# Block-masked attention with a mixture of experts behind it: earlier choice of the experts, one weight buffer split per pair

## The chip, the core and the metric

The kernel runs on one core of one Trainium2 chip. The metric is device time in microseconds (us); the median of three runs before the change is 755.88 us (754.58 to 757.23). Engines are named as in the profile: PE is TensorE, DVE is VectorE, ACT is ScalarE, POOL is GpSimd, SP is the engine whose queue issues most DMAs. L207 means line 207 of the kernel.

## The reference, cut to what matters

```python
# q, k, v: (8 batches, 8 heads, 576, 64)
scores = (1 / 8) * q @ k.T                  # per batch and head
scores = where(block_i >= block_j, scores, -1e9)        # blocks of 64, causal
attn = exp(scores - max); attn = attn / (attn.sum() + 1e-9)
x = (attn @ v)                              # as (4608, 512): a row per batch and position
logits = x @ w_gate + modality_bias[modality_id]        # 8 experts
e_idx = argmax(logits); gate_w = softmax(logits)[e_idx]
for e in range(8):                          # w1: 512 x 1024, w2: 1024 x 512 per expert
    rows = (e_idx == e)
    out[rows] = gate_w[rows] * (relu(x[rows] @ w1[e]) @ w2[e])
```

With the inputs of this problem nearly all rows go to two of the eight experts.

## The kernel before, in words

**Attention.** Two heads of a batch make a pair; there are 32 pairs, four to a batch. `run_slot` writes the order of one slot by hand, following the tuple ORDER, and every engine executes its instructions in the order in which they are written. In slot p the kernel makes for pair p the scores (S, L207, PE), the row maxima (M, L214, DVE), the exponentials (E, L227, ACT), the transposes (T, L234, PE, in six groups) and the copies of the transposes out of PSUM (C, L239; the tuple ON_DVE says which groups DVE copies, ACT copies the others). Beside this it finishes pair p-1: products with v (V, L253, PE), a copy of them (O, L261 and L262, ACT), the reciprocal of the row sums (D: `den`, L279, and L280, DVE), a turn back together with the product with w_gate (B, L273, PE), and the scaled rows (Z0 and Z1, L292 and L293, DVE). After Z1 of a batch's last pair SP stores that batch's rows (L299, eight DMAs).

**Scaling q.** q of pair p+1 is multiplied by 1/8 at "Q" of slot p: by DVE for pair 0, by ACT in one instruction for pairs from LATE = 25 on (L186), by POOL in four instructions of 144 columns for the others (L189). S of pair p+1 needs all of it. q and k of pair p+2 come with one DMA on SP's queue at "L" of slot p (L176), v of the next pair at the start of a slot (L179).

**Routing.** Z1 of a batch's last pair first empties the list `steps` of what is left in it and then fills it with the 18 steps of `routing`, small DVE instructions for the most part, with two products on PE (`total` and `counts`, only at "qp"), `biased` and `running` (only at "qv") and one exponential on ACT (`expo`). At q1 to q6 of a slot one step is executed, two in the slots 20 to 23 (slot // 4 == EARLY), and three while the next step is one of `choose`. `weight_out` turns the five sums of a partition into 80 weights (L377), which `stores` sends to `xrows` on SP. At the end five scatters per batch (L399, an indirect DMA that POOL issues) write the row numbers into `idlist`; they are made one by one at S0 and T0 of the following slots.

**Choosing two experts.** After the routing of batch EARLY - 1 = 4, 22 more DVE steps (`choose`) pick the two experts with the most rows so far, `a` and `b`, and compute where their lists begin. Of expert `a` the first 768 rows (NLEAD = 3 segments of 256) are fetched from the batches counted so far.

**Weights.** EARLY_STEPS says what is done for expert `a` before attention ends: "stage" loads a quarter of w1 or w2 (512 KB) into one of two staging buffers by SP's queue, and "prep" splits a buffer on POOL into a rounded part and a remainder, in four times a cast (L588) and a subtraction (L589) of 256 columns. "ids" and "fetch" load the list and gather the first rows. Eight buffers are split and ten staged in the slots 25 to 30.

**Experts.** The tuple LAST mixes the end of attention with the first segment's products; `run_all` then computes 18 segments, each with three fp32r products per matrix (L710 up, L756 down), ReLU and split on ACT and DVE (L716, L717), and an indirect DMA of the result (L759, POOL). `rest` would loop over what the covered segments leave.

Of the kernel before, what the change touches and what calls it, by code (L numbers as in the profile page):

```python
# [22 lines left out]
B, H, S, D = 8, 8, 576, 64  # L23
N, DM, NE, DF = 4608, 512, 8, 1024
NPAIR = B * H // 2
PPB = H // 2
NSUB = S // D
XW = 528
IW = 16
# [4 lines left out]
NROW = NE * REGION  # L34
COVER = SLOT * NSLOT
COVER_B = COVER - FEW
EARLY, NLEAD = 5, 3
LEAD = SLOT * NLEAD
BIG = float(1 << 20)
NWARM = 12  # L40
LATE = 25
SCALE = 0.125
GUARD = 1e-9
VW = D + NE
# [13 lines left out]
)  # L58
BLOCK = (12, 0, 8, 4, 16, 20)
POS = {x: BLOCK[g] + i for g, group in enumerate(GROUPS) for i, x in enumerate(group)}  # L60
ON_DVE = (0, 1, 3, 5)
SUMS = ((2, 4, 6, 5), (1, 3, 7, 8, 0))
TAILS = ((6, 3, 20, 0), (0, 5, 20, 1), (4, 2, 21, 0), (8, 4, 21, 1), (2, 1, 22, 0))
PRODUCTS = ((0, (5,)), (0, (1, 3, 7)), (0, (2, 4, 6)), (0, (8,)), (1, (4, 6, 5)), (1, (3, 7, 8)), (2, (6, 5)), (2, (7, 8)), (3, (7, 8)))
# [9 lines left out]
)  # L74

EARLY_STEPS = {
    (25, "S0"): ("stage", "stage"),
    (26, "S0"): ("prep",), (26, "T0"): ("stage", "prep"),
    (27, "S0"): ("stage", "prep"), (27, "T0"): ("stage", "prep"),
    (28, "S0"): ("ids", "stage", "prep"), (28, "T0"): ("stage", "prep"),  # L80
    (29, "S0"): ("stage", "prep"), (29, "T0"): ("stage", "prep"),
    (30, "S0"): ("fetch", "stage"), (30, "T0"): ("fetch",),
    (31, "S0"): ("fetch",), (31, "T0"): ("fetch",),
}
LAST = (
# [25 lines left out]
def attention_moe(ctx, tc, qk, vr, bkw, mid, mb, w1, w2, cf, ci, ld, out):  # L111
    nc = tc.nc
    pe, act, dve, pool = nc.tensor, nc.scalar, nc.vector, nc.gpsimd
# [64 lines left out]
    def load_v(p):  # L178
        nc.sync.dma_start(pairs[p].v.rearrange("p h a f -> p (h a f)"), vr[p])  # L179

    def scale(p):
        d = pairs[p]
        if p == 0:
            dve.tensor_scalar(d.q, d.raw[:, 0:S], SCALE, None, ALU.mult)
        elif p >= LATE:
            act.mul(d.q, d.raw[:, 0:S], SCALE)  # L186
        else:
            for i in range(0, S, 144):
                pool.tensor_scalar(d.q[:, i : i + 144], d.raw[:, i : i + 144], SCALE, None, ALU.mult)  # L189
# [46 lines left out]
    def copies(p, g):  # L236
        n = len(GROUPS[g])
        dst, src = pairs[p].pt[:, BLOCK[g] : BLOCK[g] + n].rearrange("p b c -> p (b c)"), banks[g][:, 0 : 128 * n]
        dve.tensor_copy(dst, src) if g in ON_DVE else act.copy(dst, src)  # L239

# [63 lines left out]
    def routing(b):  # L304
        xr, gl = xrs[b]
        g = Pair()
# [3 lines left out]
        def t(shape, dt=F32, **k):  # L310
            return sml.tile(shape, dt, bufs=2, **k)
# [3 lines left out]
        ix, pp, sm = (t([128, 5], name=n) for n in ("ix", "pp", "sm"))  # L315
# [58 lines left out]

        def weight_out():
            g.wt = t([128, 5, IW], name="wt")
            dve.reciprocal(g.wt, sm.unsqueeze(2).to_broadcast([128, 5, IW]))  # L377

        def stores():
            queue = nc.sync  # L380
# [12 lines left out]
        def place_sum():  # L393
# [10 lines left out]
            placing.extend((scatter, c) for c in range(5))  # L404

        return [logits, total, biased, top, shifted, hits, expo, hit_index, first, onehot, weight, weight_guard, weight_out, stores, counts, running, place_run, place_pick, place_sum]

    sel = {}
# [25 lines left out]
    def choose(eng):  # L434
        lead, start = (cst.tile([128, NE], F32, name=n) for n in ("taken", "start"))
        eng.tensor_tensor(cnt, run, bases, ALU.subtract)
        sel["oha"], sel["ea"] = pick(eng, cnt, "a", kx, ranks)
        oha = sel["oha"]
        eng.scalar_tensor_tensor(cnb, oha, -BIG, cnt, ALU.mult, ALU.add)
        eng.scalar_tensor_tensor(lead, cnt, float(LEAD), oha, ALU.min, ALU.mult)  # L440
        sel["ohb"], sel["eb"] = pick(eng, cnb, "b", kx, ranks)
        eng.tensor_tensor(rest, lead, bases, ALU.add)
        sel["ra"] = dot(eng, oha, bases, "a")
        sel["rr"] = dot(eng, oha, rest, "r")
        sel["rb"] = dot(eng, sel["ohb"], bases, "b")
        eng.scalar_tensor_tensor(begin, oha, float(COVER - LEAD), rest, ALU.mult, ALU.add)
        eng.scalar_tensor_tensor(start, sel["ohb"], float(COVER_B), begin, ALU.mult, ALU.add)
        sel["start"] = start

    def emit(name, p):  # L450
        one = {
            "L": lambda: load(p), "Q": lambda: scale(p), "V": lambda: values(p), "O": lambda: turn_out(p), "D": lambda: inverse(p), "B": lambda: back(p),
            "Z0": lambda: rows(p, 0), "Z1": lambda: rows(p, 1),
        }
        if name in one:
            one[name]()
        else:
            dict(S=scores, M=maxima, E=exps, T=transposes, C=copies)[name[0]](p, int(name[1:]))
# [36 lines left out]
    def run_slot(slot):  # L495
        nonlocal steps, ex
        if slot < NPAIR - 1:
            load_v(slot + 1)
        for name, stage in LAST if slot == NPAIR else ORDER:
            p = slot - stage  # L500
            if placing and slot < NPAIR and name in ("S0", "T0"):
                g, c = placing.pop(0)
                g(c)
            for what in EARLY_STEPS.get((slot, name), ()):
                if ex is None:
                    ex = Experts(ctx, tc, cst, scratch, btmp, con["edges"], xrows, idlist, idf, w1, w2, out, sel, run, base8, pick, dot, banks, (o0, banks[5]), placing, staging, extra, xrb)
                ex.early(what)
            if name[0:6] == "+steps":
                for f in steps[0 : int(name[6:])]:
                    f()  # L510
                steps = steps[int(name[6:]) :]
                continue
            if name[0] == "+":
                ex.early(name[1:])
                continue
            if name[0] == "q":
                kind = "" if name[1].isdigit() else name
                kinds = (kind,) if kind else ("", "c")
                quick = bool(steps) and getattr(steps[0], "kind", "") == "c"
                for _ in range(1 if kind else 3 if quick else 1 + (slot // PPB == EARLY)):  # L520
                    if slot > 1 and steps and getattr(steps[0], "kind", "") in kinds:
                        steps.pop(0)()
                continue
            if not 0 <= p < NPAIR:
                continue
            emit(name, p)
            if name == "Z1" and p % PPB == PPB - 1:
                for f in steps:
                    f()
                steps = routing(p // PPB)  # L530
                if p // PPB == EARLY - 1:
                    choose(Later(dve, steps))

    engines = {ET.PE, ET.Activation, ET.DVE, ET.Pool}
    with tc.manual_schedule(engines=engines | {ET.SP}):
        load(0)
        for _ in range(NWARM):
            pe.matmul(b0, ones, zeros, start=True, stop=True)
        nc.sync.dma_start(cft, cf)
        load(1)  # L540
        scale(0)
        load_rest()
        for slot in range(NPAIR + 1):
            run_slot(slot)
# [369 lines left out]
```

## Time and profile before

| what | value |
|---|---|
| median of three runs | 755.88 us |
| profiled execution | 752.6 us, span 751.0 us |
| mean granted PE clock | 0.99 |
| busy share of the span: PE, PEld, DVE, ACT, POOL | 97%, 84%, 49%, 43%, 30% |
| score matmuls of pair 0 and of pair 31 start at | 6.46 and 283.90 us |

The profile is of one execution. PEld is PE's loading of weights, which overlaps PE's matmuls. A row of a table by windows gives a stretch of the span, its length, the busy time of the five engines in the order PE, PEld, DVE, ACT, POOL, and then the mean granted clock of PE, the busy share of the 16 DMA engines and what they moved in GB/s. In a timeline the bracket at the end of a row tells how long the engine had been idle and what released it.

### The profile page before, as it was taken

What the parts mean: (1) busy time and instruction counts of PE and PEld (TensorE: products, weight loads), DVE (VectorE), ACT (ScalarE), POOL (GpSimd) and SP (SyncE); (2) the same over time, 40 slices, a digit from 0 to 9 for tenths busy, and PEclk for the clock granted to TensorE, in tenths of its full rate; (3) what the DMA queues carried; (4) which work ended last, traced back from release to release, by engine and by line L of the source; (5) the groups of instructions that cost most, each with busy time, mean ns of one, the idle gap of its engine ahead of it and who ended that gap; (6) DMA issues with size and microseconds to landing.
All of it is one profiled execution on the core that took longest, in us unless ns stands there. A gap on an engine that the chain in (4) does not pass through costs nothing. (4 is left out here: it accounts for less than half of the span.)

```text
span 751.0 us, 19408 instructions
## 1 busy us (share of the span) xinstructions
PE 729.0 (97%) x7800; PEld 632.7 (84%) x7800; DVE 366.9 (49%) x1068; ACT 320.9 (43%) x949; POOL 225.3 (30%) x290
## 2 busy tenths in 40 slices
PE   8999999999999998999999999999999999999995
PEld 5888888888877776987999889998899988999794
DVE  5989999999899996432220112211222122221220
ACT  5787777777766775212222122222222122221220
POOL 2223243343422984245232223322011221112101
PEclk9999999999999998999999999999999999999998
DMA  6476556463537785313220222203121221211000
GB/s 194 127 209 205 143 156 181 139 176 111 172 111 179 215 248 127 95 34 73 71 82 32 85 71 71 83 32 107 48 76 52 85 85 43 81 33 47 28 15 19
DMA packets 41916, 77.80 MB, mean 104 GB/s; under 512 B 12170, under 2 KB 24266, under 8 KB 41824
## 3 DMA queue, kind: packets, MB, share of 16 engines
q1 hardware_dynamic: 34336, 57.02, 26.2%
q0 software_dynamic: 7488, 19.52, 8.4%
q8 instruction: 62, 1.02, 0.6%
q14 instruction: 30, 0.25, 0.1%
HBM read 54.86 MB, written 22.25 MB: 103 GB/s over the span
## 5 line engine op out<-in xcount | busy, mean ns | idle before, releaser
L717 DVE SCALAR_TENSOR_TENSOR extra<-bank,extra 128x512 fp32r<-128x512 f32 x72 | 49.8, 691 | 312.4 <-ACT extra L716 312.4
L227 ACT ACTIVATE pm<-bank,nm 128x512 f32<-128x512 f32 (+3 forms) x320 | 155.6, 501 | 79.8 <-DVE nm L214 79.6
L214 DVE TENSOR_REDUCE nm<-bank 128x1 f32<-128x512 f32 (+3 forms) x320 | 120.8, 446 | 7.5 <-PE bank L207 3.7
L710 PE MATMUL bank<-extra 128*128 128x256 f32 x960 | 118.8, 284 | 2.7 <-issue 2.5
L710 PEld LDWEIGHTS bank<-extra 128*128 128x128 f32 x960 | 116.6, 190 | 4.8 <-issue 4.0
L716 ACT ACTIVATE extra<-bank 128x512 fp32r<-128x512 f32 x72 | 43.1, 598 | 157.9 <-PE bank L710 148.4
L234 PE MATMUL bank<-cf,pm 128*128 128x128 f32 (+1 forms) x736 | 91.7, 278 | 4.5 <-ACT pm L227 4.5
L710 PE MATMUL bank<-extra,w0hb 128*128 128x256 f32 x512 | 91.1, 280 | 0.0
L234 PEld LDWEIGHTS bank<-cf,pm 128*128 128x128 f32 (+1 forms) x736 | 78.1, 139 | 15.3 <-ACT pm L227 10.2
L207 PE MATMUL bank<-raw,q 64*64 64x512 f32 (+7 forms) x1280 | 88.6, 406 | 0.2 <-issue 0.2
L239 DVE COPY pt<-bank 128x512 f32<-128x512 f32 (+1 forms) x128 | 77.1, 639 | 7.7 <-PE bank L234 4.2
L710 PEld LDWEIGHTS bank<-extra,w0hb 128*128 128x128 f32 x512 | 79.0, 188 | 0.7
L253 PE MATMUL b<-pt,v 64*64 64x64 f32 (+3 forms) x896 | 77.6, 270 | 1.8 <-issue 0.9
L207 PEld LDWEIGHTS bank<-raw,q 64*64 64x64 f32 x1280 | 54.9, 133 | 28.7 <-issue 20.5
L253 PE MATMUL o<-pt,v 64*64 64x64 f32 (+3 forms) x896 | 74.5, 266 | 1.7 <-issue 1.7
L189 POOL TENSOR_SCALAR q<-raw 128x144 f32<-128x144 f32 x96 | 52.6, 576 | 75.2 <-DMA raw<-qk 62.5
L710 PE MATMUL bank<-extra,w0lb 128*128 128x256 f32 x256 | 71.8, 280 | 0.0
L399 POOL DMA_INDIRECT idlist<-idt,pi x40 | 40.0, 999 | 98.7 <-DVE pi L398 95.2
L759 POOL DMA_INDIRECT out<-scratch,ids_b x17 | 16.9, 994 | 161.9 <-ACT scratch L758 161.9
L227 ACT ACTIVATION_READ_ACCUMULATOR pm<-bank,nm 128x1 f32 x320 | 65.4, 204 | 0.0
L253 PEld LDWEIGHTS b<-pt,v 128*64 128x64 f32 (+1 forms) x896 | 54.8, 138 | 5.8 <-issue 1.9
L253 PEld LDWEIGHTS o<-pt,v 128*64 128x64 f32 (+1 forms) x896 | 52.4, 137 | 6.7 <-issue 1.7
(149 smaller groups left out, 992.6 us busy)
## 6 DMA issues: line engine op xcount, KB each, us to landing
raw<-qk SPq DMA_DIRECT2D x31, 576.0 KB
v<-vr SPq DMA_DIRECT2D x32, 384.0 KB
staging<-w SPq DMA_DIRECT2D x24, 256.0 KB
staging<-w SPq DMA_DIRECT2D x12, 512.0 KB
xrows<-xr SPq DMA_DIRECT2D x16, 256.0 KB
xrows<-xr SPq DMA_DIRECT2D x32, 128.0 KB
idlist<-btmp SPq DMA_DIRECT2D x8, 304.0 KB
xrows<-xr SPq DMA_DIRECT2D x16, 64.0 KB
```

What stands on the lines that cost most here:

```text
L189: pool.tensor_scalar(d.q[:, i : i + 144], d.raw[:, i : i + 144], SCALE, None, ALU.mult)
L207: pe.matmul(place(s, a, b)[64 * t : 64 * t + 64], d.q[hs, D * s : D * s + D], d.k[hs, a:b], start=True, stop=True)
L214: dve.tensor_reduce(d.nm[:, i : i + 1], place(s, a, b), AX.X, ALU.max, negate=True)
L227: act.activation(d.pm[:, o : o + b - a], place(s, a, b), AF.Exp, bias=d.nm[:, s : s + 1], scale=1.0, accum_out=total)
L234: pe.transpose(banks[g][0:m, 128 * i : 128 * i + 128], d.pm[:, o : o + m], idf)
L239: dve.tensor_copy(dst, src) if g in ON_DVE else act.copy(dst, src)
L253: pe.matmul(o.rearrange("p (n c) -> p n c", c=64), d.v[rows, h, block, :], x, start=start, stop=stop)
L399: last = pool.indirect_dma_start(idlist[:], bass.IndirectOffsetOnAxis(ap=g.pi[c], axis=0), g.idt[:, c, :], None, bounds_check=NROW - 1, oo ...
L710: nc.tensor.matmul(hp[:, a, :], w[:, kc, ms], x[:, kc, :], start=i == 0, stop=i == len(mm) - 1)
L716: self.nc.scalar.activation(hh, hp, AF.Relu)
L717: self.nc.vector.scalar_tensor_tensor(hl, hp, 0.0, hh, ALU.max, ALU.subtract)
L759: nc.gpsimd.indirect_dma_start(self.out, bass.IndirectOffsetOnAxis(ap=s.ids[:, s.t + i : s.t + i + 1], axis=0), yo, None, bounds_check=N - ...
```

## The change

The experts are chosen on the counts of four batches (EARLY = 4), so `choose` follows the routing of batch 3. Two steps at a place are executed in one slot alone, the slot 17. The stages and splits start in slot 21: two stages at S0 and a split at T0, then a stage and a split at T0 of each of the slots 22 to 28, and the tenth stage at S0 of slot 29; "ids" and "fetch" stay where they were. POOL scales q of every pair but the first. Group 3 of the transposes is copied by ACT. In `weight_out` DVE takes the reciprocal of five columns in place, and POOL copies them to the 80.

```diff
-EARLY, NLEAD = 5, 3
+EARLY, NLEAD = 4, 3
-LATE = 25
-ON_DVE = (0, 1, 3, 5)
+ON_DVE = (0, 1, 5)
 EARLY_STEPS = {
-    (25, "S0"): ("stage", "stage"),
-    (26, "S0"): ("prep",), (26, "T0"): ("stage", "prep"),
-    (27, "S0"): ("stage", "prep"), (27, "T0"): ("stage", "prep"),
-    (28, "S0"): ("ids", "stage", "prep"), (28, "T0"): ("stage", "prep"),
-    (29, "S0"): ("stage", "prep"), (29, "T0"): ("stage", "prep"),
-    (30, "S0"): ("fetch", "stage"), (30, "T0"): ("fetch",),
+    (21, "S0"): ("stage", "stage"), (21, "T0"): ("prep",),
+    **{(slot, "T0"): ("stage", "prep") for slot in range(22, 29)},
+    (28, "S0"): ("ids",), (29, "S0"): ("stage",),
+    (30, "S0"): ("fetch",), (30, "T0"): ("fetch",),
     (31, "S0"): ("fetch",), (31, "T0"): ("fetch",),
 }
 def scale(p):
-        elif p >= LATE:
-            act.mul(d.q, d.raw[:, 0:S], SCALE)
 def weight_out():
             g.wt = t([128, 5, IW], name="wt")
-            dve.reciprocal(g.wt, sm.unsqueeze(2).to_broadcast([128, 5, IW]))
+            dve.reciprocal(sm, sm)
+            pool.tensor_copy(g.wt, sm.unsqueeze(2).to_broadcast([128, 5, IW]))
 def run_slot(slot):
-                for _ in range(1 if kind else 3 if quick else 1 + (slot // PPB == EARLY)):
+                for _ in range(1 if kind else 3 if quick else 1 + (slot == PPB * EARLY + 1)):
```

## Rows read from the trace of the kernel before

**Rows 1.** The page: span, and busy time of PE.

```profile
span 751.0 us, 19408 instructions
...
PE 729.0 (97%) x7800; PEld 632.7 (84%) x7800; DVE 366.9 (49%) x1068; ACT 320.9 (43%) x949; POOL 225.3 (30%) x290
```

**Rows 2.** Windows, attention pairs: start:end, length, then busy time (count) per engine.

```profile
153.09:188.15 35.06, 35.06 (x639) 29.30 (x633) 33.41 (x110) 26.53 (x98) 13.76 (x21) 1.00 0.52 152
153.09:161.99 8.90, 8.90 (x171) 7.65 (x165) 8.27 (x25) 6.92 (x25) 4.21 (x6) 1.00 0.62 140
188.15:225.86 37.71, 37.07 (x638) 29.43 (x632) 34.11 (x115) 26.46 (x98) 11.63 (x17) 1.00 0.48 141
197.07:217.09 20.02, 19.38 (x327) 14.70 (x321) 17.59 (x57) 13.06 (x49) 6.42 (x10) 1.00 0.54 176
225.86:264.55 38.69, 36.47 (x639) 29.32 (x633) 37.36 (x126) 28.71 (x102) 24.44 (x43) 1.00 0.76 203
225.86:236.99 11.13, 9.35 (x171) 7.46 (x166) 10.56 (x45) 7.46 (x27) 1.96 (x2) 1.00 0.60 145
264.55:283.90 19.35, 18.39 (x326) 14.60 (x321) 18.62 (x61) 14.29 (x52) 16.41 (x29) 1.00 0.87 241
```

**Rows 3.** Windows, pair 31 and three later stretches; PEclk after POOL.

```profile
283.90:299.76 15.86, 13.31 (x173) 10.16 (x164) 9.77 (x30) 8.19 (x27) 6.84 (x7) 0.78 0.48 121
286.90:292.30 5.40, 2.85 (x21) 1.60 (x21) 1.84 (x6) 2.91 (x12) 3.31 (x4) 0.74 0.72 180
335.90:342.10 6.20, 3.62 (x16) 2.44 (x16) 0.00 (x0) 0.00 (x0) 3.88 (x5) 0.89 0.04 6
340.70:344.10 3.40, 3.16 (x13) 2.88 (x14) 0.69 (x1) 1.87 (x3) 2.15 (x2) 0.50 0.06 2
520.40:524.40 4.00, 4.00 (x37) 4.00 (x36) 0.69 (x1) 0.60 (x1) 3.04 (x3) 1.00 0.40 123
```

**Rows 4.** Timeline, DVE, pair 25: start, length, instruction.

```profile
226.89 0.49 DVE L292 TENSOR_TENSOR xr<-o,inv 128x320 f32<-128x320 f32 x1
...
229.71 1.21 DVE L214 TENSOR_REDUCE nm<-bank 128x1 f32<-128x512 f32 x2
```

**Rows 5.** Groups by line and shape: count, then busy us, mean ns.

```profile
L239 DVE COPY pt<-bank 128x512 f32<-128x512 f32 x96 | 61.8, 670 | 7.0 <-PE bank L234 3.5 <-ACT pm L227 3.5
...
L239 ACT COPY pt<-bank 128x512 f32<-128x512 f32 x64 | 35.6, 628 | 1.3 <-PE bank L234 1.3
...
L377 DVE RECIPROCAL wt<-sm 128x80 f32<-128x80 f32 x8 | 5.2, 653 | 0.3
```

**Rows 6.** Timeline, POOL: idle time before and its releaser in brackets.

```profile
207.07 2.19 POOL L189 TENSOR_SCALAR q<-raw 128x144 f32<-128x144 f32 x4
...
241.26 0.40 POOL L588 CAST extra<-staging 128x256 fp32r<-128x256 f32 x1 [1.54 <-DMA staging<-w]
...
246.11 1.01 POOL L399 DMA_INDIRECT idlist<-idt,pi  x1 [0.16 <-DVE eq L347]
247.13 0.41 POOL L588 CAST extra<-staging 128x256 fp32r<-128x256 f32 x1
```

**Rows 7.** View of line L279: duration ns min/median/max.

```profile
L279 DVE SCALAR_TENSOR_TENSOR den<-sums,long x32: 152/159/594, 21.2 to 302.3; 128x9 f32<-128x9 f32 x32
```

**Rows 8.** Timeline, SP's queue, pair 25.

```profile
227.41 6.70 SPq L299 DMA_DIRECT2D xrows<-xr  x8
...
235.51 2.60 SPq L645 DMA_DIRECT2D staging<-w  x4
238.22 0.52 SPq L176 DMA_DIRECT2D raw<-qk  x1
```

**Rows 9.** Timeline, POOL, its two long rows of indirect DMAs.

```profile
284.79 1.00 POOL L399 DMA_INDIRECT idlist<-idt,pi  x1 [0.15 <-issue]
...
290.11 1.01 POOL L671 DMA_INDIRECT xr<-xrows,row  x1 [0.30 <-issue]
...
329.36 0.98 POOL L759 DMA_INDIRECT out<-scratch,ids_lead  x1 [4.46 <-ACT scratch L758]
```

## The prediction

> **What bounds the kernel now.** I read the page first: the profiled execution took 752.6 us, 751.0 of them span, and TensorE (PE) is busy for 97% of it [rows 1]. Then I cut the attention phase at the first score matmul (L207) of each pair and read the table by windows. "Pair 17" below means the stretch from its first L207 to that of pair 18. The four pairs 17 to 20, one batch, take 35.06 us, and PE is busy for all of it; pair 17 has 8.90 of 8.90 on PE against 8.27 on DVE, 6.92 on ACT and 4.21 on POOL [rows 2]. A calm pair is thus bound by PE, with DVE close behind, and nothing that only unburdens DVE or ACT can shorten it. What can be had is what the other pairs take above this batch: pairs 21 to 24 take 37.71, pairs 25 to 28 take 38.69, and pairs 29 and 30 take 19.35 where two calm ones take 2 x 8.90 = 17.8 [rows 2]. That is 2.65 + 3.63 + 1.55 = 7.8 us in all. Last, pair 31 takes 15.86 us at a mean clock of 0.78 [rows 3], some 7.2 above a calm pair of 8.6.
>
> **The change, part by part.**
>
> *Choice on four batches.* Counted from the reference's inputs, four batches give expert 6 1114 rows and expert 1 1026, five give 1396 and 1320, all eight 2289 and 2153. The same two are chosen, 768 lead rows exist either way, and 2304 and 2176 rows cover both. The expert phase therefore does the same work, and I book nothing for it. The 22 small DVE steps of choose() move four pairs forward. Three places of the pair before take nine; thirteen are still left when Z1 of the batch's last pair empties the list. Today they stand between Z1 and the first maximum: Z0 starts at 226.89, the maximum at 229.71 [rows 4], and pair 25 takes 11.13 where pair 17 took 8.90, 2.23 more. This burst now falls on pair 21. The copy that leaves DVE lets Z0 start about 0.6 earlier (it waits for the matmuls of back() then), so 1.65 stays.
>
> *Two steps at a place.* The old condition held in pairs 20 to 23. It brought weight() right behind expo(), whose result ACT delivers late, and pairs 22 and 23 take 20.02 us [rows 2], some 2.5 above two calm ones. The new condition holds in pair 17 alone, where only logits() can run before total() needs its own place: it does nothing. The 2.5 us go.
>
> *Third group's copy to ACT.* 0.67 us a pair leaves DVE, 0.63 comes to ACT [rows 5]. ACT is busy 6.92 of 8.90, and the copy follows the second group's; the bank is wanted only by the late scores of the next pair. I price it at 0 in calm pairs (bounds: -0.3 us a pair, about half of what leaves DVE, and +0.6, if all of it stood before PE).
>
> *Reciprocal.* 80 columns take 0.65 us [rows 5]; five cost no more, so at most 0.65 x 8 = 5 us of DVE is saved, and 0 of the end in calm pairs. The copy on POOL is not in the trace; by POOL's 0.40 us for 256 columns and 0.55 for 144 [rows 6] I take 0.4. SP's weight store waits for it, and behind that store stand the loads of the next pair; they have a pair's time to spare.
>
> *One buffer a pair, and scaling stays on POOL.* Today two buffers are split in each of the pairs 26 to 29, and DVE pays: den (L279), 0.159 in the median, takes up to 0.594 [rows 7]. The excess of pairs 26 to 30 is mostly this. Now eight buffers go over pairs 21 to 28, and those pairs should fall to calm ones; for what contention remains I add 0.5 in all (bounds 0 and 8 x 0.4). On this rests a rule of the Trainium skill, page "SBUF — State Buffer", section "Who interferes with whom": a DVE instruction with two SBUF inputs and a GpSimd (POOL) instruction that reads SBUF block each other, whoever comes second. It speaks against spreading the work over twice the pairs; the trace agrees that den is stretched under a split. By it alone each of eight pairs would pay for its two-input DVE instructions; that is a rival below.
>
> POOL's order in pair 21 is: scatter, scale(22), scatter, first split; in pair 22: scatter, scale(23), scatter, split. POOL takes them in that order, and the first split waits for its weights. In today's pair 25 SP first issues eight stores (6.70 us from 227.41), then the four weight DMAs from 235.51, then raw [rows 8]; the split starts at 241.26 after a wait for that DMA [rows 6], 15.4 us after the pair's start. Today ACT scales there, so nobody minds. In the new kernel SP has the same list in pair 21. With the stores 0.6 earlier the split starts at 14.8, that is 14.8 - (8.90 + 1.65) = 4.3 into pair 22. The split takes 4.7 (241.26 to 245.95), the scatter behind it 1.2 (to 247.13), scale 2.2 [rows 6]: scale(23) ends at 12.4, where pair 22 should have ended at about 9.0. The scores of pair 23 wait 3.4 us, with PE idle. This is a new stall. Such a pause is also followed by half clock in this trace: PE was busy 2.85 of the 5.40 us from 286.90, at a mean granted clock of 0.74, and after a like stretch 340.70 to 344.10 stands wholly at 0.50, the lower level of 1.2 GHz [rows 3]. From this last one, the shortest, I add half of 3.4 = 1.7 (bounds 0 and 3.4).
>
> After that POOL needs per pair 4.7 + 2.2 + 1.2 for each of on average 1.25 scatters, 8.4 of 8.8 us: just enough. In pair 29 one weight DMA pair and eight stores stand before raw(31) on SP; scaling on POOL is 1.5 us longer than one ACT instruction, and I add 0.5 (bounds 0 and 2.8).
>
> *Sum, pairs 21 to 30.* 35.06 + 1.65 + 3.4 + 1.7 for 21 to 24, 35.06 for 25 to 28, 17.8 + 0.5 for 29 and 30, contention 0.5: 95.7, against 37.71 + 38.69 + 19.35 = 95.75 today. The gains are eaten by the stall.
>
> *Pair 31.* From 286.90 on PE's matmuls come in short bursts though they wait for nothing, and the clock goes down. In the same microseconds POOL works off five indirect DMAs in a row, 284.79 to 291.12, which the splits had held up [rows 9]. The other such stretch of PE, 335.90 to 342.10 (3.62 of 6.20 busy) [rows 3], lies under POOL's only other row of more than three, nine DMAs from 329.36 [rows 9]. Rows of three leave PE untouched: 4.00 of 4.00 busy at clock 1.00 [rows 3]. I have no mechanism, only this coincidence. In the new kernel the last split is over by pair 29, the scatters are made as they fall due, and only a row of three is left in pairs 30 and 31. I take the 7.2 us as gone (bounds 0 and 7.2).
>
> Sum: 752.6 - 0.1 - 7.2 = 745.3. The profiled execution stands 3.3 below the median of 755.88, so I predict 755.88 - 7.3 = **748.6**.
>
> **The rivals.**
>
> *The bursts of PE stay, or come elsewhere.* For: nothing explains them. Against: they fall together with the two long POOL rows. Then 755.8.
>
> *Slower: POOL does not keep up.* Place: scale(p+1) behind the split of the pair before. It decides from the point where POOL's work for a pair exceeds PE's 8.8; a tenth more than 8.4, where DVE blocks it, makes each of pairs 23 to 29 late by some 0.5 and drops the clock once more, 5 us; with PE's bursts kept, 755.8 + 5 = 761. Against: today's splits run at the same speed beside a busier DVE.
>
> *No stall at pair 23, the bursts gone.* If the weights land while pair 21 still runs, 3.4 + 1.7 fall away: 743.5. Against: SP's eight stores.
>
> *The splits slow every one of the eight pairs.* den stands between two of DVE's copies, and where DVE has no slack its 0.594 - 0.159 = 0.4 reach the end: 8 x 0.4 - 0.5 = 2.7 more, 751.3. Against: the copy that left DVE frees 0.6 just there.
>
> *DVE, not PE, sets the calm pair.* Then the copy moved is worth 0.3 us in each of 32 pairs: about 739. Against: PE busy 8.90 of 8.90.
>
> **How the numbers follow.** Forecast 0.44, bursts stay 0.24, POOL late 0.13, no stall 0.08, eight slow pairs 0.07, DVE bound 0.04. A measurement tells about 0.3%, 2.3 us, from no change. Faster takes the forecast, no stall, eight slow pairs, DVE bound and 0.01 of "bursts stay": 0.64. Within 0.3%: 0.16 of "bursts stay". Slower: POOL late and the 0.07 left of "bursts stay", 0.20. The forecast's own range is 745 to 753; with the rivals, 743 to 760.
>
> **What would show it.** Right: a POOL wait of several us for staging before the first split, then a PE gap of about 3.4 before the scores of pair 23, half clock behind it; pairs 24 to 28 at 8.6 to 9.0; pair 31 at about 8.6 with full clock; the same expert phase. Wrong: PE gaps before every pair's scores (POOL late), no gap at pair 23, or pair 31 still near 15.9.

## The result, and the profile after

The changed kernel takes 747.58 us (median of 4 runs, 747.08 to 749.92) against 756.05 for the kernel before on the same chip: ratio 0.9904, interval [0.9881, 0.9928]. 748.6 was predicted, 743 to 760 as the range. The profiled execution took 747.08 us, of which 745.4 is span. From the page, the lines that answer to [rows 1], and the granted clock in 40 slices:

```profile
span 745.4 us, 19432 instructions
PE 724.3 (97%) x7800; PEld 633.5 (85%) x7800; DVE 345.0 (46%) x1036; ACT 332.2 (45%) x974; POOL 242.6 (33%) x326
PEclk9999999999999999998999999999999999999998
```

The windows, with columns as in [rows 2]: half clock in pair 0; pairs 0 to 15, 17 to 20, 21 to 24, 21 alone, 22 alone, 23 with 24, 25 to 28, 29 with 30, 31; and two stretches behind the attention, the first under the end of POOL's row of nine indirect DMAs (PE busy 4.79 of 6.80 us), the second at half clock behind it.

```profile
12.10:15.30 3.20, 3.20 (x16) 2.36 (x18) 1.00 (x2) 2.24 (x7) 1.30 (x3) 0.50 0.33 123
5.96:145.62 139.66, 137.88 (x2400) 114.59 (x2403) 119.46 (x381) 112.39 (x401) 47.92 (x81) 0.99 0.56 168
154.17:189.26 35.09, 35.09 (x639) 29.43 (x634) 31.43 (x112) 28.48 (x102) 14.02 (x22) 1.00 0.54 152
189.26:228.84 39.58, 35.59 (x639) 29.16 (x633) 34.17 (x125) 28.37 (x102) 27.69 (x48) 1.00 0.72 201
189.26:200.02 10.76, 9.28 (x172) 7.38 (x166) 9.64 (x43) 7.32 (x27) 4.21 (x6) 1.00 0.64 153
200.02:211.69 11.67, 9.16 (x171) 7.30 (x161) 9.71 (x35) 7.68 (x27) 7.56 (x13) 1.00 0.95 270
211.69:228.84 17.15, 17.15 (x311) 14.48 (x315) 14.82 (x47) 13.37 (x49) 15.91 (x29) 1.00 0.61 184
228.84:264.42 35.58, 35.26 (x638) 29.36 (x632) 32.17 (x106) 28.36 (x102) 31.52 (x55) 1.00 0.72 209
264.42:283.29 18.87, 18.23 (x328) 15.18 (x320) 16.29 (x57) 14.94 (x53) 11.96 (x19) 1.00 0.66 183
283.29:293.88 10.59, 9.65 (x166) 7.99 (x158) 8.06 (x28) 7.40 (x26) 4.41 (x5) 1.00 0.26 60
326.80:333.60 6.80, 4.79 (x36) 4.46 (x36) 0.83 (x3) 0.14 (x1) 5.10 (x6) 0.94 0.03 6
332.90:339.70 6.80, 5.50 (x23) 5.23 (x24) 1.38 (x2) 2.03 (x3) 5.07 (x6) 0.50 0.09 3
```

Against the windows of before: pairs 17 to 20 +0.03 us (35.09 for 35.06), 21 to 24 +1.87, 25 to 28 -3.11, 29 and 30 -0.48, pair 31 -5.27 (10.59 for 15.86). Pair 16 starts 1.09 later (145.62 for 144.53): pairs 0 and 1, with the half clock from 12.10 to 15.30, take 1.5 longer, and pair 0 starts 0.5 earlier (5.96 for 6.46). Some 0.3 are lost behind the attention. The sum is -5.6, the difference of the two spans; the rest of the 8.5 us between the medians is that the profiled execution of before (752.6) stood 3.4 below the median of 756.05 and this one only 0.5 below its own.

Where pair 22 loses its time can be read on three engines. First POOL, from the first split on (times start, length, instruction, idle time before and its releaser):

```profile
203.56 0.39 POOL L584 CAST extra<-staging 128x256 fp32r<-128x256 f32 x1 [5.15 <-DMA staging<-w]
...
207.50 0.73 POOL L585 TENSOR_TENSOR extra<-staging,extra 128x256 fp32r<-128x256 f32 x1
208.39 1.02 POOL L395 DMA_INDIRECT idlist<-idt,pi  x1 [0.16 <-DMA raw<-qk]
209.45 2.19 POOL L184 TENSOR_SCALAR q<-raw 128x144 f32<-128x144 f32 x4
```

The split waits 5.15 us for its weights, then come split, scatter and scale(23), which ends at 211.64. The split ends at 208.23; POOL's next idle time, the 0.16 before 208.39, ends with the landing of raw(23). So split and load are over at nearly the same time, and without the split scale(23) could have started only about 1 us earlier. PE's first scores of pair 23 stand right behind it:

```profile
211.69 1.08 PE L202 MATMUL bank<-raw,q 64*64 64x512 f32 x8 [2.51 <-POOL q L184]
```

And SP's queue in pairs 21 and 22, which answers to [rows 8]: eight stores, then four weight loads, then raw(23), the last of these rows, which goes out 0.9 us into pair 22.

```profile
190.42 6.42 SPq L294 DMA_DIRECT2D xrows<-xr  x8
...
198.24 2.60 SPq L641 DMA_DIRECT2D staging<-w  x4
200.94 0.52 SPq L173 DMA_DIRECT2D raw<-qk  x1
```

DVE in pair 21, as in [rows 4]: from Z0 to the first maximum.

```profile
189.90 0.49 DVE L287 TENSOR_TENSOR xr<-o,inv 128x320 f32<-128x320 f32 x1
...
192.74 0.69 DVE L209 TENSOR_REDUCE nm<-bank 128x1 f32<-128x512 f32 x1
```

Three views by line (ns, minimum/median/maximum): den, which answers to [rows 7], the reciprocal of five columns, and the copy on POOL.

```profile
L274 DVE SCALAR_TENSOR_TENSOR den<-sums,long x32: 150/160/652, 22.2 to 296.4; 128x9 f32<-128x9 f32 x32
L372 DVE RECIPROCAL sm<-sm x8: 190/191/192, 72.6 to 318.4; 128x5 f32<-128x5 f32 x8
L373 POOL COPY wt<-sm x8: 239/248/276, 72.8 to 319.0; 128x80 f32<-128x80 f32 x8
```

### The profile page after: what moved, and what is told of

It is laid out like the page before. It is cut to its first block, busy times and chain, and to the rows that moved or that the text cites. A ratio compares the mean times of both kernels' runs of the same rounds, so it can differ in the third digit from the quotient of the medians.

```text
span 745.4 us, 19432 instructions
## 1 busy us (share of the span) xinstructions
PE 724.3 (97%) x7800; PEld 633.5 (85%) x7800; DVE 345.0 (46%) x1036; ACT 332.2 (45%) x974; POOL 242.6 (33%) x326
## 5 line engine op out<-in xcount | busy, mean ns | idle before, releaser
L184 POOL TENSOR_SCALAR q<-raw 128x144 f32<-128x144 f32 x124 | 67.7, 573 | 59.4 <-PE bank L229 47.9
L248 PE MATMUL o<-pt,v 64*64 64x64 f32 (+3 forms) x896 | 72.5, 262 | 1.0 <-issue 1.0
L234 DVE COPY pt<-bank 128x512 f32<-128x512 f32 (+1 forms) x96 | 59.2, 642 | 21.2 <-PE bank L229 15.6
L752 PE MATMUL o<-extra 128*128 128x512 f32 x240 | 57.2, 394 | 0.0
```

The costliest lines, as they stand in the source:

```text
L248: pe.matmul(o.rearrange("p (n c) -> p n c", c=64), d.v[rows, h, block, :], x, start=start, stop=stop)
L752: nc.tensor.matmul(y, s.hs[m][x][:, ts], self.part(w, 1, m // 2)[:, m % 2, :], start=n == 0, stop=n == len(mm) - 1)
```

## The experiments

They ran on four chips, told apart by the time of the kernel before: 740.0 on chip A, 754.8 on B, 740.7 on C, 740.0 on D. The chip of the prediction (756) behaves like B and may be B. "Bursts" are the short runs of PE's matmuls with gaps between them in which PE waits for nothing that the trace shows. The runs of one chip were made close together in time, so they can't tell the chip from a passing state of it.

**Both kernels again.** No edit. What was expected counts on chip A; they ran on chip B.

> The kernel before, unchanged, on a chip on which it takes 740.0 us (756.0 where the prediction was made). Theory 1, the prediction's: five indirect DMAs in a row on POOL are enough to break up PE's matmuls; then pair 31 takes about 15.9 here too, and PE has gaps under the row of nine. Theory 2: the row of nine is there in all four kernels run on this chip, and PE has no gap under it; the bursts belong to the chip, pair 31 takes under 11, and most of the 16 us between the chips is these bursts, in pair 31, behind the row of nine and in the shorter stretches of 0.2 in routing pairs.

Measured: 755.0. Pair 31 takes 15.44, and five indirect DMAs stand close together on POOL at its start, the fifth after 0.98. Windows: pair 31, and the stretch under the end of the row of nine.

```profile
285.70:301.14 15.44, 13.46 (x174) 8.94 (x165) 10.21 (x32) 7.82 (x27) 6.11 (x6) 0.89 0.45 117
337.30:343.00 5.70, 2.97 (x15) 2.13 (x14) 0.00 (x0) 0.00 (x0) 3.71 (x4) 0.82 0.04 7
```

It repeats what was seen before, so by this chip alone theory 1 would stand; it falls with two runs on chip A and one on chip C, below.

> The changed kernel, unchanged, on the chip of the experiments. Theory: without PE's bursts in pair 31 there is nothing to win there; what stays is that pairs 25 to 30 are shorter and pairs 21 to 24 longer by the stall: 735.9 (scaling of pair 23 on ACT) + 2.6 = 738.5, ratio to before 0.998, where it was 0.990. Half clock behind the stall in some executions, 740 then. Rival: the gain holds here too, 732.8.

Measured on chip B: 748.04 (746.24 to 749.62), ratio 0.9902 [0.9878, 0.9927]: the result repeats. Its profile has the same stall (PE gap 3.02 us before the scores of pair 23), and now half clock behind it. Pair 23, and the half-clock stretch in it:

```profile
212.11:222.39 10.28, 10.28 (x156) 8.32 (x159) 7.09 (x20) 7.09 (x25) 9.65 (x18) 0.83 0.54 151
212.70:216.10 3.40, 3.40 (x37) 2.13 (x28) 1.91 (x4) 1.79 (x7) 3.14 (x7) 0.50 0.24 78
```

10.28 against 8.59 in the first profile of the changed kernel, where the clock stayed at 1.00: the half clock costs 1.7 us when it comes.

**Scaling of pair 23 on ACT (chip A).**

```
         if p == 0: ...
+        elif p == 23:
+            act.mul(d.q, d.raw[:, 0:S], SCALE)
```

> The changed kernel with one edit: the scaling of pair 23 on ACT, all others stay on POOL. Theory: the PE gap of 2.51 us before the scores of pair 23 is scale(23), queued on POOL behind the first split, which waits for its weights. Then pair 22 falls from 11.68 to about 8.9 us and the time from 747.6 to about 744.8. Rival: the scores wait for raw(23), which lands late behind SP's stores and weight loads; then the gap stays and the time stays at 747.6. Second rival: the instruction makes ACT late instead, 0.4 us back.

Measured: 735.93 against 740.04, ratio 0.9949 [0.9931, 0.9968]; pair 22 takes 8.91 and PE has no gap before the scores of pair 23.

```profile
199.05:207.96 8.91, 8.91 (x170) 7.18 (x163) 8.40 (x30) 6.78 (x26) 4.62 (x9) 1.00 0.95 283
```

The time came as by the first theory: the gap is scale(23), late on POOL. What makes it late, the split or the load of raw(23) that the rival names, this edit does not tell: ACT starts at 207.22 and needs 0.68 us, so on ACT the scaling is in time even behind a late load. The splits moved by a pair, below, tell them apart. The same run decides about the bursts. POOL's row of nine is there, dense as ever, and under it PE is busy all the time at full clock, where [rows 3] has 3.62 of 6.20 under the end of that row:

```profile
317.87 0.99 POOL L757 DMA_INDIRECT out<-scratch,ids_lead  x1 [4.20 <-ACT scratch L756]
...
328.11 0.97 POOL L397 DMA_INDIRECT idlist<-idt,pi  x1 [0.30 <-issue]
```

```profile
317.87:329.10 11.23, 11.23 (x98) 11.23 (x97) 5.20 (x30) 3.40 (x6) 8.77 (x9) 1.00 0.09 28
```

**Old plan of loads and splits (chip A).** EARLY_STEPS and the scaling on ACT from pair 25 as in the kernel before, all else as changed.

> The changed kernel with the plan of the weight loads and splits, and the scaling on ACT from pair 25, as before the change; the choice stays on four batches, the copy on ACT, five reciprocals. Theory: the stall before pair 23 goes (-2.8), pairs 26 to 30 are long again (+3.1 and +0.5), POOL's row of five indirect DMAs in pair 31 and PE's bursts come back (+5.3): 753.7. Rival (the gain of the change came from the other edits): 747.6 or below.

Measured: 738.78 against 740.04, ratio 0.998 [0.997, 0.999]. The windows 21 to 24, 25 to 28, 29 with 30, and pair 31:

```profile
188.58:225.51 36.93, 35.44 (x638) 29.09 (x633) 33.14 (x125) 28.41 (x102) 11.87 (x18) 1.00 0.49 145
225.51:262.75 37.24, 36.26 (x638) 29.48 (x633) 32.66 (x104) 30.93 (x106) 23.96 (x42) 1.00 0.75 205
262.75:282.31 19.56, 18.48 (x329) 14.91 (x320) 18.29 (x64) 15.33 (x54) 16.66 (x28) 1.00 0.85 249
282.31:291.83 9.52, 9.52 (x158) 7.57 (x158) 6.90 (x23) 8.71 (x29) 7.54 (x10) 1.00 0.59 154
```

The stall is gone (36.93). Pairs 25 to 30 are long again, but by 1.7 and 0.7 us against the changed kernel's 35.58 and 18.87, where 3.1 and 0.5 were expected: the burst of `choose`, 2.2 us in pair 25 of the kernel before, stays in pair 21 here. Pair 31 is not long: five indirect DMAs stand in a row in it, and PE is busy for 9.52 of 9.52.

```profile
283.69 1.01 POOL L399 DMA_INDIRECT idlist<-idt,pi  x1 [0.15 <-issue]
...
289.01 1.01 POOL L671 DMA_INDIRECT xr<-xrows,row  x1 [0.31 <-issue]
```

So the term of 5.3 us for the bursts does not exist on this chip, and without it the old plan costs little: 0.998 here against 0.9965 for the kernel nearest to the change on chip C, below.

**POOL held back in pair 29 (chip C).**

```
+    (29, "T0"): ("hold",),    # 18 scalings of a spare tile on POOL
+        elif p == 31: act.mul(d.q, d.raw[:, 0:S], SCALE)
...                            # hold and its tile are left out here
```

> The changed kernel with POOL kept busy by 18 scalings of a spare 128x144 tile (about 9.9 us) at the end of pair 29, so that five indirect DMAs queue up and are then made in a row in pairs 30 and 31, as in the kernel before; the scaling of pair 31 moves to ACT so that the scores don't wait for it. Theory (the row on POOL brings PE's bursts, on a chip that has them): pair 31 goes from 10.4 to 14 to 16 us, time from 748 to about 752. Rival (the late splits or the loads of the kernel before did it): pair 31 stays at 10 to 11, time 748. On a chip without bursts: no change against the changed kernel.

Measured: 736.49 against 740.68, ratio 0.995 [0.9936, 0.9964]. The row is there, six indirect DMAs from 282.88 to 290.70 with one small copy between, and PE does not break up under it. POOL, and the window of the row:

```profile
270.94 11.72 POOL L618 TENSOR_SCALAR idle<-idle 128x144 f32<-128x144 f32 x18
282.88 1.02 POOL L397 DMA_INDIRECT idlist<-idt,pi  x1 [0.22 <-issue]
...
289.67 1.03 POOL L677 DMA_INDIRECT xr<-xrows,row  x1 [0.16 <-issue]
```

```profile
280.50:290.00 9.50, 9.50 (x160) 7.50 (x150) 7.84 (x28) 8.38 (x28) 7.64 (x11) 1.00 0.22 62
```

**The row of nine spread out (chip C).**

```
         g, c = self.placing.pop(0)
         g(c)
+        self.hold(2)          # two scalings of a spare tile on POOL
...                            # hold and its tile are left out here
```

> The changed kernel with 1.1 us of other work on POOL (two scalings of a spare tile) behind each of the eight list scatters that today stand in a row behind the attention, so that each starts 2.4 us after the other instead of 1.28. Theory (dense rows of indirect DMAs break up PE's matmuls): PE's gaps under the row (2.4 to 2.7 us) and the half clock behind them (6.8 us) go, time from 748.0 to about 743.5. Rival 1 (each indirect DMA costs PE the same, however far apart): the gaps stay, 748. Rival 2: the ids come 9 us later and the row gathers that need them make PE wait, 750. On a chip without bursts: no change.

Measured: 737.74, ratio 0.9965 [0.9953, 0.9977]. A chip without bursts, so it tells nothing of what spacing does to them. It serves another end: up to the end of the attention it is the changed kernel, and it is the nearest there is to that kernel's time on such a chip. Pair 22 takes 11.96 and pair 31 8.80.

**Copy back on DVE (chip A).** `ON_DVE = (0, 1, 3, 5)`.

> The changed kernel with one edit: the third group's copy goes back to DVE. Theory (PE sets a calm pair): 747.6 within 1 us; calm pairs stay at 35.1 for four, the wait for the first maximum in pair 21 grows by up to 0.6. Rival (DVE sets the calm pair): 0.3 us in each of 32 pairs, about 757. Rival on the other side: on ACT the copy makes every fourth pair 0.1 longer (8.72 where it was 8.61), so 0.8 us comes back, 746.8.

Measured: 740.27, ratio 1.0001 [0.9992, 1.0011]. Pairs 17 to 20 and pair 21:

```profile
153.70:188.59 34.89, 34.89 (x638) 29.10 (x633) 33.06 (x115) 26.42 (x98) 14.03 (x22) 1.00 0.53 152
188.59:199.93 11.34, 9.35 (x171) 7.39 (x166) 10.77 (x45) 6.82 (x25) 4.21 (x6) 1.00 0.60 146
```

Four calm pairs take 34.89 here and 34.90 in the kernel with the scaling of pair 23 on ACT: the copy is worth nothing there. Pair 21 is 0.58 longer than that kernel's 10.76, as expected. How much of the ratio is the copy can't be said: this profile has half clock in pair 23 (10.18 us), and the nearest changed kernel ran on another chip.

**Two steps at a place in pairs 20 to 23 (chip A).** `1 + (slot // PPB == 5)`.

> The changed kernel with two steps at a place in pairs 20 to 23, as before the change. Theory: weight() stands right behind expo() again, pairs 22 and 23 are together 2.5 us longer, and four of the thirteen steps of the burst in pair 21 are taken earlier (-0.5): 749.6. Rival: the stall before pair 23 hides that wait, since scores are late anyway: 747.6 or 747.1.

Measured: 740.33, ratio 1.0006 [0.9991, 1.002]. Pair 21 takes 10.89, pair 22:

```profile
199.34:211.58 12.24, 9.16 (x172) 7.30 (x163) 11.03 (x39) 7.68 (x27) 7.58 (x13) 1.00 0.89 263
```

That is 0.3 more than the 11.96 of the kernel with the spread row, with 0.1 more in pair 21, not 2.5: beside the stall the early weight() costs little. The rival was nearer; the ratio holds half clock in pair 23 (10.29 us) too. What the edit brings in a kernel without the stall was not tried.

**Burst spread over pair 20, scaling of pair 23 on ACT (chip B).** `else (5 if slot == 20 else 3) if quick`, with the edit of pair 23.

> The changed kernel with the scaling of pair 23 on ACT and, in pair 20, five steps of the choice at a place instead of three. Theory: six of the thirteen steps leave the burst that delays the first maximum of pair 21, the PE gap of 1.48 there shrinks to about 0.7: 735.9 - 0.8 = 735.1. Rival: DVE has no room for the six steps in pair 20, whose time grows by as much: 735.9.

Measured: 745.75, ratio 0.988 [0.9856, 0.9904]. Pair 21, which starts at 189.57, still takes 10.76. DVE from Z0 to the first maximum:

```profile
191.16 0.49 DVE L289 TENSOR_TENSOR xr<-o,inv 128x320 f32<-128x320 f32 x1
...
193.04 1.81 DVE L211 TENSOR_REDUCE nm<-bank 128x1 f32<-128x512 f32 x4
```

The maximum starts 3.47 us into the pair, as before (192.74 - 189.26 = 3.48). Only Z0 starts later (1.59 into the pair for 0.64). DVE has no idle time between, so moving steps about ahead of the maximum did not help. The rival's result holds, but not its reason: pair 20 takes 8.55 as before, and the steps pile up ahead of Z0 of pair 21. The later Z0 has a price of its own. The stores behind it begin 2.10 us into pair 21 instead of 1.16, raw(23) leaves SP 1.93 us into pair 22 instead of 0.92, ACT waits for it, PE stands still for 0.56, and pair 22 takes 9.72 where the kernel with this scaling on ACT alone took 8.91:

```profile
209.32 0.68 ACT L183 ACTIVATE q<-raw 128x576 f32<-128x576 f32 x1 [0.75 <-DMA raw<-qk]
```

**Splits one pair later (chip B).** First split in pair 22, the others in 23 to 29; the first two loads stay in pair 21.

> The changed kernel with all eight splits one pair later (pairs 22 to 29 instead of 21 to 28), the first two weight loads still in pair 21. Theory: the weights have landed before the first split, scale(23) is not held up, no PE gap before the scores of pair 23: 738.5 - 2.6 = 735.9, like the kernel with that scaling on ACT. Rival: POOL falls behind at the other end, scale(31) or the row gathers wait for the last split, and pairs 30 and 31 give back 1 to 3 us: 737 to 739.

Measured: 745.52, ratio 0.9877 [0.9848, 0.9906]. Pair 22 takes 10.62, not 8.9, and PE's gap before the scores of pair 23 is 1.46, where the changed kernel has 3.02 on this chip. The split is out of the way, and scale(23) still waits, now for its own load:

```profile
208.69 0.57 POOL L184 TENSOR_SCALAR q<-raw 128x144 f32<-128x144 f32 x1 [5.66 <-DMA raw<-qk]
```

```profile
210.92 1.07 PE L202 MATMUL bank<-raw,q 64*64 64x512 f32 x8 [1.46 <-POOL q L184]
```

So the load alone, without the split, leaves about half of the stall.

**Loads half a pair later as well (chip C).**

```
-    (21, "S0"): ("stage", "stage"), (21, "T0"): ("prep",),
-    **{(slot, "T0"): ("stage", "prep") for slot in range(22, 29)},
+    (21, "T0"): ("stage", "stage"), (22, "T0"): ("prep",),
+    **{(slot, "T0"): ("stage", "prep") for slot in range(23, 30)},
```

> Splits one pair later, as in the kernel with the splits in pairs 22 to 29, and the first two weight loads also half a pair later, behind the load of raw(23) on SP. Theory: the 1.45 us of PE gap that were left there (POOL waited 5.66 us for raw(23), which stood behind the weight loads) go too, pair 22 falls from 10.62 to about 8.9; time 745.5 - 1.7 = 743.8. Rival: raw(23) waits for the eight stores ahead of it and not for the weights, and nothing changes, 745.5; or the first split now waits for its weights, POOL falls behind, 747.

Measured: 734.46, ratio 0.9922 [0.9909, 0.9935], 3.3 below the spread-row kernel of the same chip. SP issues raw(23) at 196.31, ahead of the weight loads (197.45) and 2.4 us before pair 22, where it went out at 201.23, 0.9 us into the pair, with the loads ahead of it. From its issue to the start of scale(23) it is 7.4 us here and 7.5 there: what moved is the issue. Scale(23) now starts at 203.71, in pair 22, which takes a calm pair's time:

```profile
203.71 2.19 POOL L184 TENSOR_SCALAR q<-raw 128x144 f32<-128x144 f32 x4 [2.26 <-DMA raw<-qk]
```

```profile
198.72:207.62 8.90, 8.90 (x170) 7.17 (x166) 7.99 (x30) 6.77 (x26) 4.62 (x8) 1.00 1.03 276
```

So the stall had two causes, side by side: the split ahead of scale(23) on POOL, and the weight loads ahead of raw(23) on SP. The late load alone leaves 1.46 us of it; the split alone, with raw(23) in time, was not run. With scaling on ACT the second hid on chip A, since ACT needs 0.68 us where POOL needs 2.19; in the kernel with the spread burst, where raw(23) goes out a microsecond later, 0.56 us of it were left.

**Loads later and the row spread (chip D).** The last two edits together.

> The kernel with the first weight loads half a pair later and the splits one pair later (ratio to before 0.992 on a chip without bursts), and 1.1 us of other POOL work behind each of the eight scatters of the row. On a chip with bursts (before at about 755): if dense rows of indirect DMAs are what breaks up PE there, the first two expert turns fall from 58 to about 52 us and the time is 743.8 - 5 = 739; if not, 58 us stay, with PE gaps under the wider row, 743.8. On a chip without bursts (before at about 740): 52 us either way, time 734.5.

Measured: 734.51 against 740.03, ratio 0.993 [0.9916, 0.9943]. Pair 22 takes 8.88, so the stall is gone a second time. Again a chip without bursts: whether spacing the row ends them stays untried on a chip that has them.

## Why the prediction was right, and where by luck

- *Calm pairs, copy, reciprocal.* Right: 35.09 for 35.06 in the same four pairs. The reciprocal fell to 0.19 us, the copy on POOL takes 0.25 (0.4 estimated); neither shows in a calm pair. No run changes them alone.
- *The burst moves to pair 21.* Right: 10.76 against 8.93 for the pair before the change, 1.83 (1.65 predicted). That the copy on ACT takes 0.6 off it is shown: with the copy back on DVE the pair takes 11.34.
- *The new stall.* Right in place and kind, a little large. Predicted: split at 14.8 into pair 21, scale(23) over at 12.4 into pair 22, 3.4 lost. Measured: 203.56 - 189.26 = 14.3, 211.64 - 200.02 = 11.6, and 11.67 - 8.88 (the like pair 18) = 2.8 lost. Incomplete in cause: taking the split away alone leaves 1.46 us of PE gap, because raw(23) stands behind the weight loads on SP. The prediction read that order in [rows 8] but gave the load no time to land; for the loads behind the weight store it said that they have a pair's time to spare. In pair 22 raw(23) landed only when the split was done (POOL's row at 208.39).
- *Half clock behind the stall, 1.7.* Right in size, not in certainty. It is absent in the profiled execution (17.15 for pairs 23 and 24). Of the six profiles with this stall it came in three (the repeat on chip B, the copy on DVE, the two steps), with gaps of 3.02, 2.20 and 3.08 us; it did not after 2.51, 2.79 and 2.19. Where it came, pair 23 took 10.2 to 10.3 for 8.59. It should have been a rival's difference, not a sure term.
- *Eight splits at the price of calm pairs.* Right: 35.58 for 25 to 28, 0.5 above 35.09. The Trainium skill (page "SBUF — State Buffer", section "Who interferes with whom") lets a DVE instruction with two SBUF inputs and a POOL instruction that reads SBUF block each other; the trace agrees, den still takes up to 0.652, at 207.60 under the last subtraction of the first split. But it rarely falls there: four of its 32 executions take over 0.2 us. And pairs 23 and 24, split in each, take 17.15 together, so the rival with eight slow pairs falls. POOL keeps up.
- *Pairs 29 and 30.* 18.87 for 18.3, with pair 30 the long one (10.10); 0.58 us of it are two gaps of PE without a releaser in the trace.
- *Pair 31, the largest term.* 5.27 of the 7.2 came. 2 us of it stay (10.59, PE busy 9.65), with a row of only three on POOL: from 283.41 to 287.15 PE is busy for 3.20 of 3.74 us, so the reading that rows of three leave PE untouched was wrong for this place. And the reason given, "only this coincidence", is not enough: on chips A and C rows of five, six and nine leave PE whole. What is shown: the bursts come on chip B and on the chip of the prediction, in pair 31 and under the row of nine in both kernels, and not on A and C with the same rows; on D no such row was profiled, and only the 740.0 of the kernel before puts it with A and C. What stays open is what makes such a chip different, why the change left only a part of the bursts in pair 31, and whether thinning the rows would help there. The five microseconds are real on the chip of the prediction; on chip A pair 31 takes 9.52 with the old plan and 8.80 with the new one. The changed kernel itself was not run without bursts. The kernel that is the changed one up to the end of the attention gains about a third there: 0.9965 on chip C. That the term came in at this size is luck: the choice of chip, which the prediction did not know of, decided it.
- *The sum.* 745.3 was predicted for the profiled execution, 747.08 came. Pair 31 is 1.9 above its forecast, pair 0 with its half clock 1.1 (it came in eight of the twelve profiles of the changed kernel and its variants and in neither of the two of before; whether the change favours it is open), pairs 29 and 30 some 0.6, the part behind the attention 0.3; pairs 21 to 24 are 2.2 below, for want of the half clock and with a shorter stall. The misses up and down cancel in part. The median came nearer, 747.58 for 748.6, because the 3.3 us between the profile and the median of before did not repeat (0.5 here). That part of the agreement is luck.

## What to carry over

When a transfer or a piece of background work is moved forward, write down for every queue that it now stands in what comes behind it: here the weight loads held up raw(23) on SP, and the split held up scale(23) on POOL, and taking away the split alone won back about half. Place such a load behind the loads that the next stage needs; with the splits one pair later, that made the best version, 0.992 of before where the kernel nearest to the change gives 0.9965 on the same chip. And a loss in which an engine waits for nothing that the trace shows is worth a run on another chip before a term is built on it.

## What was not expected of the hardware

The same kernel, the one before the change, takes 740 to 741 us on three chips, 754.8 on chip B and 756 where the prediction was made. No profile of it was kept on a chip of the first kind, so the parts of the difference are read from kernels with the same stretches. Calm pairs are the same (8.55). Most of the difference is PE breaking up, with half clock behind it: pair 31 (15.4 us, against 9.5 on chip A for the kernel with the old plan and the same row on POOL) and the first expert turns (PE busy 2.97 of 5.70 us against 11.23 of 11.23). A routing pair differs by 0.2 us (pair 17: 8.93 against 8.73), with PE busy throughout on both kinds of chip.
